# Plain attention pairs whose value product is turned round, and weight words that are joined from contiguous operands

## Chip, core and metric

The kernel runs on one core of a Trainium2 chip. The metric is the device time of one execution in microseconds (us), and the median of three runs is what counts. The profile is one execution of the same program, so every duration below belongs to that execution.

## What is computed

Attention over 4 batches, 8 heads, 768 positions and a head size of 64, in which a query sees the first 4 keys and the 128 keys that end at its own position, followed by a feed-forward block over all 3072 tokens:

```python
def _attn_ref(q, k, v, n_sink, window):
    scores = np.matmul(q, k.transpose(0, 1, 3, 2)) / np.sqrt(D)
    keep = is_sink | in_window
    scores = np.where(keep, scores, -1000000000.0)
    a = np.exp(scores - np.max(scores, axis=-1, keepdims=True))
    a = a / (np.sum(a, axis=-1, keepdims=True) + 1e-09)
    return np.matmul(a, v)

def _moe_ref(x, w_in, w_out):            # 512 -> 2048 -> 512
    h = x @ w_in
    g = h * np.clip(h + 3.0, 0.0, 6.0) / 6.0
    return g @ w_out
```

The feed-forward weights arrive as 64-bit floats, the rest as 32-bit floats.

## The kernel before

**Tiling.** The tokens are cut into 12 units of 256 (4 batches, 3 units each). The four units that begin a batch come first, as units 0 to 3. Of a unit, attention is done for one pair of heads at a time, so there are 48 pairs. The first 14 pairs are "plain": their products run on 32-bit floats as they are. All other products use a float split into a high and a low part, and three products of the parts.

**A plain pair** `s` goes through these steps, and each has a letter. `S` computes the scores of two query tiles (`t`) for both heads (`h`) on TensorE. `M` (line 370) applies the mask on VectorE (DVE) and finds the row's least value. `X` (line 404) takes the exponential on ScalarE (ACT), which also adds up each row by an accumulator. `R` (lines 409 and 410) adds 1e-9 to the two sums of a head and inverts them on DVE. `N` (lines 395 and 397) scales the 128x128 or 128x256 block of probabilities by the inverse, on DVE, or on ACT where the string `NORM0` says so (only for `h` = `t` = 1). `T` (line 443) transposes three 128x128 blocks on TensorE and `C` copies them to SBUF (DVE or ACT by the string `PFE`). `E` (line 495) multiplies with the values: the values are the stationary operand, padded with zeros to 128 columns so that both heads add up in one tile `av` of 128 features by 256 tokens, and the probabilities move past. `x` and `y` (lines 552 and 556) write the high and low part of `av`, the input of the feed-forward block.

**The weights.** Each of the 16 halves of weight tiles (`W`, `w`) arrives as pairs of 32-bit words and is put together into floats of 128x1024 in six steps: ACT takes the high words (1) and the low words (2), DVE joins them in two bitwise instructions (3, line 199, and 4, line 202), then the high part is copied (5, ACT or DVE) and the low part is subtracted (6, line 207, DVE). Before, step 2 writes back in place, so both joins read and step 3 writes every second 32-bit word.

**The feed-forward block** of a unit has 8 slices: `F` (line 576, 24 matmuls a slice in two halves), `G` (four steps on ACT and DVE that end in line 603) and `O` (line 618, 12 matmuls in two halves).

**The order.** A long string `FIRST` lists, step by step, the first part of the program: pairs 0 to 11, pair 12 up to `C`, all 16 weight halves, and the feed-forward blocks of units 0 and 1. Each engine executes its steps in that order. After it comes a loop over the other pairs that spreads the feed-forward work of the other units between their steps. `keep_busy` (step `i`, line 86) issues matmuls that compute nothing; ten stand at the program's start and 17 more in `FIRST`. PSUM tiles come from a pool of eight banks.

Of the kernel before, what the change touches and what calls it, by code (L numbers as in the profile page):

```python
# [44 lines left out]
def attn_ffn_kernel(ctx: ExitStack, tc: tile.TileContext, qx, kx, vx, px, vsx, limits, w_in, w_out, out):  # L45
# [127 lines left out]
    def W_decode(j, step):  # L173
# [14 lines left out]
        if step == 1:  # L188
# [21 lines left out]
    GHF = "DDDDADDADADDDAAD"  # L210
    WHI = "AAAADDAAADAAAAAD"
# [45 lines left out]
    PFE = "AAADAAADADAAAAAAAADADADAAA"  # L257
    XHF = "DAAAAAAAADAAA"
# [4 lines left out]
    homes = {}  # L263

    def A_lent(s):
# [4 lines left out]
        nc.sync.dma_start(out=home, in_=px[b, p])  # L270
        st_[s].update(kr=home[:, 0:256], qr=home[:, 256:512],
                      VS=home[:, 512:1024].rearrange("p (t h d) -> p t h d", t=2, h=2))
# [9 lines left out]
    def A_v(s):  # L282
        b, u, p = pus[s]
        n = 3 if u else 2
        if plain(s):
            VS = work.tile([P, 2, 2, 2 * D], F32, tag="VS", name="VF")
            nc.sync.dma_start(out=VS.rearrange("p t h d -> p (t h d)"), in_=px[b, p][:, 512:1024])
# [103 lines left out]
    NORM0, NORM = "AADDAAAADAADA", "AAAA"  # L391
# [9 lines left out]
    def X_exp(s, h, t):  # L401
        d, i = st_[s], 2 * h + t
        blk = cell(s, h, t, 0, spans(pus[s][1])[t][1])
        nc.scalar.activation(out=blk, in_=blk, func=AF.Exp, scale=-1.0,  # L404
                             bias=d["nb"][:, i:i + 1], accum_out=d["sm"][:, i:i + 1])

# [4 lines left out]

    def N_plain(s, h, t):
        i = 2 * h + t
        norm(NORM0[s % len(NORM0)] if i == 3 else "D", cell(s, h, t, 0, spans(0)[t][1]), st_[s]["rc"][:, i:i + 1])

    def C_soft(s, h):
# [3 lines left out]
        for t in range(2):  # L420
            X_exp(s, h, t)
        R_sums(s, h)
# [67 lines left out]
    def E_plain(s, h):  # L490
        d = st_[s]
        if h == 0:
            d["av"] = ps.tile([P, UT], F32, tag="bank", name="av")
        for slot, c, o0 in ((0, 0, 0), (1, 2 * P, P)):
            nc.tensor.matmul(out=d["av"][:, o0:UT], lhsT=d["VS"][:, slot, h, :], rhs=d["pf"][:, h, c:c + UT - o0],  # L495
                             start=(h == 0 and slot == 0), stop=(h == 1 and slot == 1))

    def E_av(s, h):
# [4 lines left out]
        if plain(s):  # L503
            E_plain(s, h)
            if h == 1:
                x_high(s, d["av"])
                x_low(s, d["av"])
# [150 lines left out]
    def drain(n):  # L658
# [15 lines left out]
        p.0 p.1 W.0 p.2 p.3 W.1 p.4 p.5 p.6 S.0.0 p.7 S.0.1 M.0.0.0 W.2 M.0.1.0 X.0.0.0 M.0.0.1 S.1.0 W.3 S.1.1  # L674
        i.10 X.0.1.0 M.0.1.1 X.0.0.1 M.1.0.0 m W.4 M.1.1.0 M.1.0.1 W.5 X.0.1.1 R.0.0 l.8 X.1.0.0 M.1.1.1 X.1.0.1
        N.0.0.0 N.0.0.1 R.0.1 X.1.1.0 T.0.0 R.1.0 N.0.1.1 N.0.1.0 N.1.0.0 N.1.0.1 X.1.1.1 T.0.1 T.1.0 C.0.0
        R.1.1 C.0.1 E.0.0 N.1.1.0 N.1.1.1 w.0.1 S.2.0 S.2.1 M.2.0.0 E.0.1 M.2.1.0 w.0.2 M.2.0.1 M.2.1.1 S.3.0
        x.0 X.2.0.0 S.3.1 w.0.3 X.2.0.1 T.1.1 i.7 X.2.1.0 X.2.1.1 R.2.0 M.3.0.0 C.1.0 N.2.0.0 N.2.0.1 X.3.0.0
        R.2.1 E.1.0 w.1.1 M.3.0.1 N.2.1.0 T.2.0 N.2.1.1 M.3.1.0 T.2.1 M.3.1.1 X.3.0.1 S.4.0 y.0 X.3.1.0 C.1.1
        S.4.1 X.3.1.1 R.3.0 E.1.1 M.4.0.0 w.1.2 N.3.0.0 N.3.0.1 R.3.1 T.3.0 M.4.0.1 C.2.0 N.3.1.0 S.5.0 N.3.1.1  # L680
        C.2.1 M.4.1.0 E.2.0 M.4.1.1 X.4.0.0 w.0.4 X.4.0.1 T.3.1 X.4.1.0 E.2.1 X.4.1.1 R.4.0 W.6 M.5.0.0 S.5.1
        x.1 N.4.0.0 x.2 C.3.1 C.3.0 y.2 X.5.0.0 S.6.0 y.1 E.3.0 w.0.5 N.4.0.1 R.4.1 M.5.0.1 T.4.0 N.4.1.0
        N.4.1.1 E.3.1 M.5.1.0 M.5.1.1 X.5.0.1 T.4.1 w.1.3 x.3 S.6.1 C.4.0 X.5.1.0 S.7.0 y.3 X.5.1.1 C.4.1 E.4.0
        w.2.2 R.5.0 R.5.1 N.5.0.0 N.5.0.1 E.4.1 N.5.1.1 N.5.1.0 M.6.0.0 w.3.2 M.6.0.1 T.5.0 M.6.1.0 T.5.1
        M.6.1.1 S.7.1 w.0.6 x.4 C.5.0 C.5.1 E.5.0 X.6.0.0 y.4 X.6.0.1 w.1.4 F.0.0.0 X.6.1.0 X.6.1.1 R.6.0 W.7
# [292 lines left out]
```

## Time and profile before

| | |
|---|---|
| median of 3 runs | 667.37 us (665.54 to 667.58) |
| the profiled execution's own time | 666.84 us |
| its span in the trace | 665.0 us |
| TensorE matmul (PE) busy | 652.1 us, 98% of the span |
| VectorE (DVE) busy | 516.0 us, 78% |
| ScalarE (ACT) busy | 413.2 us, 62% |
| chain of work that ended last | PE 83%, DVE 14% |

A matmul's busy time runs to its modelled end, and matmuls overlap: a matmul of 256 columns is shown with some 277 ns, although the next one starts much sooner. So the busy share of PE says little, and the pace, from start to start, says how much work PE has. The same holds on DVE and ACT to a smaller degree. The chain of waits, which is printed in order of time, shows such paces.

### The profile page before, as it was taken

To read this page: it belongs to the slowest core of one execution; us is meant where nothing else is said; L and a number is where in the kernel's file an instruction comes from. 1 tells how busy PE (TensorE), PEld (TensorE's weight loads), DVE (VectorE), ACT (ScalarE), POOL (GpSimd) and SP (SyncE) were. 2 spreads that over 40 slices of the span, in tenths; PEclk is the share of its full clock that TensorE was granted. 3 is DMA by queue.
4 is the path that set the end of the run, shared out by engine and by line. 5 is a ranking of instruction groups with operands and counts; after the bars stand their busy time and mean duration, and the time that the engine had idled before them with its cause. 6 is when DMAs were issued, how large, how long until landed. Compare 5 with 4: busy or idle time off the path is not lost.

```text
span 665.0 us, 13749 instructions
## 1 busy us (share of the span) xinstructions
PE 652.1 (98%) x4594; PEld 611.8 (92%) x4594; DVE 516.0 (78%) x1433; ACT 413.2 (62%) x1042; POOL 181.1 (27%) x336
## 2 busy tenths in 40 slices
PE   9999999999999999999999999999999999999995
PEld 7779889889999999999999999999999999999994
DVE  6999999656779878887887887977986987875431
ACT  6997795365566666666666567667666666662211
POOL 1000000000034353344433533443443435332000
PEclk9999999999999999999999999999999999999998
DMA  8940750045455545455456446545544454420001
GB/s 332 380 160 32 285 222 17 17 131 136 122 144 142 147 121 151 114 143 162 119 123 171 110 119 167 132 110 146 145 129 131 126 146 121 108 66 1 33 1 36
DMA packets 47646, 86.45 MB, mean 130 GB/s; under 512 B 7632, under 2 KB 31952, under 8 KB 45520
## 3 DMA queue, kind: packets, MB, share of 16 engines
q1 hardware_dynamic: 47568, 85.49, 44.2%
q8 instruction: 39, 0.64, 0.4%
q14 instruction: 39, 0.32, 0.1%
HBM read 42.99 MB, written 6.29 MB: 74 GB/s over the span
## 4 chain that ended last, share of the span: by engine, by line
PE 83%; DVE 14%; issue 1%; ACT 0%; POOL 0%; POOLq 0%; ACTq 0%
PE hps L576 34%; PE o L618 34%; PE av L524 6%; PE sp L388 5%; DVE wt L202 3%; PE pt L461 2%; DVE w L207 2%; DVE lent L199 2%; DVE Ph L370 2%; DVE Ph L397 1%; DVE g L603 1%; DVE st L199 1%; PE av L495 1%; DVE gf L594 1%; PE idle L86 1%
## 5 line engine op out<-in xcount | busy, mean ns | idle before, releaser
L576 PE MATMUL hps<-x,w 128*128 128x256 f32 x2304 | 282.4, 277 | 2.0 <-ACT pf L35 0.9
L576 PEld LDWEIGHTS hps<-x,w 128*128 128x128 f32 x2304 | 269.4, 192 | 5.8 <-ACT pf L35 1.3
L618 PE MATMUL o<-w,gh 128*128 128x512 f32 x768 | 234.0, 386 | 0.0
L428 POOL TENSOR_TENSOR Pt<-Pt 128x256 f32<-128x256 f32 x64 | 53.9, 842 | 355.1 <-ACT Pt L404 355.1
L618 PEld LDWEIGHTS o<-w,gh 128*128 128x128 f32 x768 | 139.6, 197 | 9.9 <-issue 0.7
L618 PE MATMUL o<-w,g 128*128 128x512 f32 x384 | 145.9, 380 | 1.0 <-DVE g L603 0.8
L589 ACT ACTIVATE gf<-hps,three 128x512 f32<-128x512 f32 x96 | 66.3, 691 | 82.6 <-PE hps L576 82.4
L594 DVE SCALAR_TENSOR_TENSOR gf<-gf,hps 128x512 f32<-128x512 f32 x96 | 66.5, 695 | 35.7 <-ACT gf L589 34.0
L618 PEld LDWEIGHTS o<-w,g 128*128 128x128 f32 x384 | 75.4, 196 | 9.6 <-DVE g L603 2.1
L474 POOL TENSOR_SCALAR_AFFINE_SELECT ph<-ph 128x256 fp32r<-128x256 f32 x128 | 63.7, 498 | 41.0 <-ACT ph L35 41.0
L404 ACT ACTIVATE Pt<-Pt,nb 128x272 f32<-128x272 f32 (+2 forms) x136 | 69.9, 514 | 8.0 <-DVE nb L370 7.4
L395 ACT ACTIVATE Pt<-Pt,rc 128x144 f32<-128x144 f32 (+2 forms) x136 | 49.3, 410 | 35.8 <-DVE rc L410 34.6
L476 POOL TENSOR_SCALAR_AFFINE_SELECT ph<-ph 128x256 fp32r<-128x256 f32 x128 | 64.9, 507 | 23.0 <-DVE ph L30 17.6
L370 DVE CUSTOM_DVE_ANT_0 Pt<-sp,m_t 128x272 f32<-128x272 f32 x128 | 53.2, 433 | 22.9 <-PE sp L388 18.7
L603 DVE TENSOR_TENSOR g<-gf,gh 128x512 fp32r<-128x512 f32 x96 | 69.2, 723 | 1.0
L30 DVE TENSOR_TENSOR kt<-kr,kt 128x400 fp32r<-128x400 f32 (+1 forms) x34 | 21.9, 643 | 27.5 <-DMA out_dram<-ost 14.6
L388 PE MATMUL sp<-K 128*128 128x272 f32 (+2 forms) x272 | 42.6, 279 | 0.0
L524 PE MATMUL av<-ph,VS 128*128 128x256 f32 x268 | 40.9, 275 | 0.0
L41 DVE CAST gh<-gf 128x512 fp32r<-128x512 f32 x91 | 39.6, 436 | 1.3
L388 PEld LDWEIGHTS sp<-K 128*128 128x128 f32 x272 | 38.3, 190 | 1.2
L409 DVE TENSOR_SCALAR sm<-sm 128x2 f32<-128x2 f32 x96 | 32.9, 343 | 7.4 <-ACT Pt L404 6.8
L30 DVE TENSOR_TENSOR ph<-pt,ph 128x256 fp32r<-128x256 f32 (+1 forms) x68 | 29.0, 426 | 11.4 <-ACT ph L35 10.9
(95 smaller groups left out, 794.4 us busy)
## 6 DMA issues: line engine op xcount, KB each, us to landing
K<-kt SPq DMA_DIRECT2D x128, 200.0 KB, 3.5
K<-kt SPq DMA_DIRECT2D x136, 64.0 KB, 2.5
kr<-in_kx_dram SPq DMA_DIRECT2D x32, 200.0 KB, 2.5
out_dram<-ost SPq DMA_DIRECT2D x48, 128.0 KB, 2.1
vr<-in_vx_dram SPq DMA_DIRECT2D x32, 192.0 KB, 2.6
lent<-in_w_in_dram SPq DMA_DIRECT2D x5, 1024.0 KB, 10.6
lent<-in_w_out_dram SPq DMA_DIRECT2D x5, 1024.0 KB, 12.4
qr<-in_qx_dram SPq DMA_DIRECT2D x40, 128.0 KB, 2.3
```

What stands on the lines that cost most here:

```text
L370: nc.vector.tensor_tensor_reduce(out=cell(s, h, t, 0, w), in0=sp[:, 0:w], in1=m[:, 0:w], scale=-SCALE, scalar=3.0e38, op0=ALU.add, op1=ALU ...
L388: nc.tensor.matmul(out=sp[:, 0:w], lhsT=Q[:, h, t * P:(t + 1) * P], rhs=keys, start=(r == 0), stop=(r == 1))
L404: nc.scalar.activation(out=blk, in_=blk, func=AF.Exp, scale=-1.0, bias=d["nb"][:, i:i + 1], accum_out=d["sm"][:, i:i + 1])
L428: nc.gpsimd.tensor_tensor(out=both, in0=both, in1=prior, op=ALU.add)
L474: nc.gpsimd.affine_select(out=prior[i], in_=own[i], pattern=[[0, 2], [-1, P]], base=0, channel_multiplier=1, compare_op=ALU.is_gt, fill=0.0)
L476: nc.gpsimd.affine_select(out=own[i], in_=own[i], pattern=[[0, 2], [1, P]], base=0, channel_multiplier=-1, compare_op=ALU.is_ge, fill=0.0)
L524: nc.tensor.matmul(out=o, lhsT=l, rhs=r, start=(j == 0), stop=(j == len(seq) - 1))
L576: nc.tensor.matmul(out=hp[:, half, :], lhsT=l(i)[:, c, fs], rhs=r, start=(c == 0 and j == 0), stop=(c == NP - 1 and j == 2))
L589: nc.scalar.activation(out=gf, in_=hp, func=AF.Relu, bias=three, scale=1.0)
L594: nc.vector.scalar_tensor_tensor(out=gf, in0=gf, scalar=6.0, in1=hp, op0=ALU.min, op1=ALU.mult)
L603: eng(GLO, state["n"] * NP).tensor_tensor(out=g, in0=gf, in1=gh.bitcast(F32), op=ALU.subtract)
L618: nc.tensor.matmul(out=acc, lhsT=l[:, f, tt::2], rhs=r(i)[:, f, :].rearrange("p (s d) -> p d s", s=2), start=(i == 0 and f == 0 and j == 0 ...
```

## The change

The change has three parts and a new table.

1. For plain pairs the transposed probabilities become the stationary operand of `E`, and the values move: 65 columns for one head, the 65th being all ones, so that column 64 of the result is the row's sum. The exponential no longer accumulates. `R` now runs once for a pair, on the four sums in PSUM. A new step `U` scales the result (128x256) by the inverses on DVE, and a new step `V` transposes it back on TensorE (two 128x128 blocks into a PSUM tile `xp`), from which `x` and `y` read. `N` is gone. The packed input of a pair is 772 words wide instead of 1024, and for pairs 0 and 1 it is loaded in two pieces (`q`, `u`).
2. Of the weights, step 1 keeps the sign of the high word (`Copy` for `Abs`), step 2 writes to a contiguous tile `last`, and both joins read and write contiguous words. `last` lies in the second half of the place that the finished weights will take.
3. `FIRST` is written anew, without step `i`. It holds the same pairs, weight halves and feed-forward slices as before. The strings that choose engines change too: over the plain pairs `x` stands on DVE for 8 instead of 3, and one copy of each kind (`C`, weight step 5, `G` step 3) changes sides.

```diff
-            nc.scalar.activation(out=d["it"].bitcast(F32), in_=high.bitcast(F32), func=AF.Abs, scale=2.0 ** -112)
+            nc.scalar.activation(out=d["it"].bitcast(F32), in_=high.bitcast(F32), func=AF.Copy, scale=2.0 ** -112)
...
-            nc.scalar.activation(out=low, in_=low.bitcast(U32), func=AF.Copy, scale=2.0 ** -29 * (1 - 2.0 ** -18),
-                                 bias=7.5 * 2.0 ** -18 - 0.5)
+            d["last"] = lent(NW - 1 - j, I32)[:, PW:2 * PW]
+            nc.scalar.activation(out=d["last"], in_=low.bitcast(U32), func=AF.Copy,
+                                 scale=2.0 ** -29 * (1 - 2.0 ** -18), bias=7.5 * 2.0 ** -18 - 0.5)
         elif step == 3:
-            nc.vector.scalar_tensor_tensor(out=low, in0=high, scalar=-2 ** 31, in1=low,
+            nc.vector.scalar_tensor_tensor(out=d["last"], in0=d["it"], scalar=-2 ** 31, in1=d["last"],
                                            op0=ALU.bitwise_and, op1=ALU.bitwise_or)
         elif step == 4:
-            nc.vector.scalar_tensor_tensor(out=d["it"], in0=d["it"], scalar=3, in1=low,
+            nc.vector.scalar_tensor_tensor(out=d["it"], in0=d["it"], scalar=3, in1=d["last"],
                                            op0=ALU.logical_shift_left, op1=ALU.bitwise_or)
...
-    PFE = "AAADAAADADAAAAAAAAADADADAAA"
-    XHF = "DAAAAAAAADAAA"
+    PFE = "DAAAADDADAAAAAAAADAAAAADAA"
+    XHF = "DDDAADDDAAAA"
...
+    def R_plain(s):
+        d = st_[s]
+        nc.vector.tensor_scalar(out=d["sm"], in0=d["av"][:, :, D], scalar1=1e-9, scalar2=None, op0=ALU.add)
+        nc.vector.reciprocal(out=d["rc"], in_=d["sm"])
+
+    def U_plain(s):
+        d = st_[s]
+        d["rows"] = work.tile([P, 2, 2, D], F32, tag="tmp", name="rows", bufs=1)
+        nc.vector.tensor_tensor(out=d["rows"].rearrange("p t h d -> p h t d"),
+                                in0=d["av"][:, :, 0:D].rearrange("p (h t) d -> p h t d", h=2),
+                                in1=d["rc"].rearrange("p (h t) -> p h t", h=2).unsqueeze(3).to_broadcast([P, 2, 2, D]),
+                                op=ALU.mult)
+
+    def V_plain(s):
+        d = st_[s]
+        d["xp"] = ps.tile([P, UT], F32, tag="bank", name="xp")
+        for t in range(2):
+            nc.tensor.transpose(out=d["xp"][:, t * P:(t + 1) * P],
+                                in_=d["rows"][:, t].rearrange("p h d -> p (h d)"), identity=ident)
...
-    def N_plain(s, h, t):
-        i = 2 * h + t
-        norm(NORM0[s % len(NORM0)] if i == 3 else "D", cell(s, h, t, 0, spans(0)[t][1]), st_[s]["rc"][:, i:i + 1])
...
-            d["av"] = ps.tile([P, UT], F32, tag="bank", name="av")
-        for slot, c, o0 in ((0, 0, 0), (1, 2 * P, P)):
-            nc.tensor.matmul(out=d["av"][:, o0:UT], lhsT=d["VS"][:, slot, h, :], rhs=d["pf"][:, h, c:c + UT - o0],
-                             start=(h == 0 and slot == 0), stop=(h == 1 and slot == 1))
+            d["av"] = ps.tile([P, 4, D1], F32, tag="bank", name="av")
+        for t in range(2):
+            for slot in range(t + 1):
+                c = (t + slot) * P
+                nc.tensor.matmul(out=d["av"][:, 2 * h + t, :], lhsT=d["pf"][:, h, c:c + P], rhs=d["VS"][:, slot, h, :],
+                                 start=(slot == 0), stop=(slot == t))
...
     FIRST = """
-        p.0 p.1 W.0 p.2 p.3 W.1 p.4 p.5 p.6 S.0.0 p.7 S.0.1 M.0.0.0 W.2 M.0.1.0 X.0.0.0 M.0.0.1 S.1.0 W.3 S.1.1
+        q.0 q.1 p.2 u.1 u.0 v.9 W.2 p.3 p.4 S.0.0 W.0 S.0.1 M.0.0.0 p.5 S.1.1 M.0.1.0 X.0.0.0 M.0.1.1 S.1.0
...
```

The program's order, on TensorE behind the ten `idle` matmuls at the start, where the scores of pairs 0 and 1 end. `idle` are matmuls that compute nothing, `sp` are scores, `pt` the transposed probabilities (`Ph`); `lent` and `ident_r` hold a pair's inputs and the identity. Before:

```order
L357 MATMUL sp_148<-lent_108 128x256
L357 MATMUL sp_150<-lent_108 128x256
L86 MATMUL idle_152<-ident_r_72 128x128 x10
L443 MATMUL pt_198<-ident_r_72,Ph_132 128x128 x3
L443 MATMUL pt_209<-ident_r_72,Ph_132 128x128 x3
```

After, at the same place:

```order
L359 MATMUL sp_145<-lent_108 128x128
L359 MATMUL sp_147<-lent_108 128x128
L466 MATMUL pt_163<-ident_r_72,Ph_132 128x128 x3
L466 MATMUL pt_178<-ident_r_72,Ph_132 128x128 x3
L359 MATMUL sp_184<-lent_111 128x256
L359 MATMUL sp_186<-lent_111 128x256
```

The ten `idle` matmuls ahead of the first transposes are gone, so the transposes stand right behind the scores.

On DVE, where one pair's sums stand among the work of others (`nb` holds a pair's least values, `sm` and `rc` its sums and their inverses, `pf` the copied transposes, `av` the product with the values, `rows` the scaled product; `st` holds the words of a weight half as they were loaded). Before, with pairs 6 and 7:

```order
L202 SCALAR_TENSOR_TENSOR wt_292<-wt_292,st_116 128x1024
L409 TENSOR_SCALAR sm_449<-sm_449 128x2
L410 RECIPROCAL rc_450<-sm_449 128x2
L370 ISA Ph_502,nb_503<-sp_426,m_00_100 128x128
L370 ISA nb_503 128x1
L397 TENSOR_SCALAR Ph_447<-Ph_447,rc_450 128x128
L397 TENSOR_SCALAR Ph_447<-Ph_447,rc_450 128x256
```

After, with pairs 3, 4 and 6:

```order
L41 COPY pf_384<-pt_335 128x384
L414 TENSOR_SCALAR sm_279<-av_341 128x4
L415 RECIPROCAL rc_280<-sm_279 128x4
L200 SCALAR_TENSOR_TENSOR lent_333<-wt_352,lent_333 128x1024
L420 TENSOR_TENSOR rows_408<-av_341,rc_280 128x2x2x64
L203 SCALAR_TENSOR_TENSOR wt_352<-wt_352,lent_333 128x1024
L372 ISA Ph_420,nb_421<-sp_389,m_00_100 128x128
```

The two sums of one head, with the scaling of its probabilities behind them, have become four sums that are read from the product `av`, with one scaling of that product behind them. The joins read and write `wt` and `lent` (which is `last` here), both contiguous, where one of them read `st`, of which it took every second word.

On TensorE, where the products of a pair stand among the work of others. Before, with pairs 1 to 5:

```order
L495 MATMUL av_289<-pf_282,lent_108 128x256
L495 MATMUL av_289<-pf_282,lent_108 128x128
L443 MATMUL pt_334<-ident_r_72,Ph_277 128x128 x3
L357 MATMUL sp_342<-lent_118 128x128
L357 MATMUL sp_344<-lent_118 128x128
L495 MATMUL av_349<-pf_339,lent_113 128x256
L495 MATMUL av_349<-pf_339,lent_113 128x128
```

After, with pairs 3 to 6 (`xp` are the new transposes of step `V`):

```order
L520 MATMUL av_341<-lent_111,pf_327 128x65 x3
L359 MATMUL sp_379<-lent_167 128x256
L359 MATMUL sp_381<-lent_167 128x256
L359 MATMUL sp_387<-lent_167 128x128
L359 MATMUL sp_389<-lent_167 128x128
L466 MATMUL pt_394<-ident_r_72,Ph_364 128x128 x3
L520 MATMUL av_400<-lent_120,pf_384 128x65 x3
L466 MATMUL pt_404<-ident_r_72,Ph_364 128x128 x3
L520 MATMUL av_400<-lent_120,pf_384 128x65 x3
L429 MATMUL xp_414<-ident_r_72,rows_408 128x128 x2
```

A product of one head has three matmuls of 65 columns instead of one of 256 and one of 128. Between the last product of pair 3 (`av_341`) and its transposes back (`xp_414`) stand scores, transposes and products of later pairs.

## Rows read from the trace of the kernel before

**Rows 1.** Busy time in stretches: start:end, length; PE, PEld, DVE, ACT, POOL busy (instructions); PEclk, DMA share, GB/s.
```profile
6.00:26.00 20.00, 19.75 (x146) 16.12 (x147) 17.82 (x93) 19.02 (x60) 0.20 (x1) 1.00 1.02 424
26.00:46.00 20.00, 18.71 (x122) 14.78 (x119) 19.73 (x70) 19.82 (x54) 0.00 (x0) 1.00 0.50 195
86.00:106.00 20.00, 19.11 (x125) 16.43 (x123) 19.93 (x35) 15.59 (x23) 0.00 (x0) 1.00 0.37 143
```

**Rows 2.** Chain of waits in order of time: start us, us, engine, tile, line, count.
```profile
104.92 1.14 DVE w L207
106.10 5.40 PE hps L576 x46
```

**Rows 3.** Groups by line and form, 0 to 230 us: busy us, mean ns, idle before.
```profile
L207 DVE TENSOR_TENSOR w<-wt,w 128x1024 fp32r<-128x1024 f32 x16 | 20.2, 1277 | 0.0
L199 DVE SCALAR_TENSOR_TENSOR lent<-lent 128x1024 int32<-128x1024 int32 x10 | 14.2, 1448 | 0.0
L202 DVE SCALAR_TENSOR_TENSOR wt<-wt,lent 128x1024 int32<-128x1024 int32 x10 | 13.8, 1414 | 0.0
L404 ACT ACTIVATION_READ_ACCUMULATOR Ph<-Ph,nb 128x1 f32 x56 | 11.4, 203 | 0.0
L397 DVE TENSOR_SCALAR Ph<-Ph,rc 128x128 f32<-128x128 f32 x26 | 7.2, 280 | 0.1
L397 DVE TENSOR_SCALAR Ph<-Ph,rc 128x256 f32<-128x256 f32 x17 | 5.9, 347 | 0.0
L395 ACT ACTIVATE Ph<-Ph,rc 128x256 f32<-128x256 f32 x11 | 5.5, 503 | 0.4 <-DVE rc L410 0.3
```

**Rows 4.** DVE in order of time: start us, us, line, operation, tiles, count.
```profile
28.23 0.15 DVE L409 TENSOR_SCALAR sm<-sm 128x2 f32<-128x2 f32 x1
28.42 0.17 DVE L410 RECIPROCAL rc<-sm 128x2 f32<-128x2 f32 x1
28.50 0.72 DVE L397 TENSOR_SCALAR Ph<-Ph,rc 128x128 f32<-128x128 f32 x3
```

**Rows 5.** Chain of waits: pieces on DVE, which show its paces.
```profile
14.41 1.22 DVE st L199
16.10 0.46 DVE Ph L397 x2
18.19 0.34 DVE x L556
18.52 0.47 DVE pf L41
46.44 2.70 DVE lent L199 x2
89.82 0.60 DVE w L41
```

**Rows 6.** Chain of waits: pieces on PE, which show its paces.
```profile
130.80 0.65 PE av L495 x4
136.09 2.60 PE o L618 x12
142.12 0.66 PE pt L443 x6
142.78 2.68 PE hps L576 x24
145.46 0.86 PE sp L357 x8
159.12 0.63 PE sp L388 x6
```

**Rows 7.** PE in order of time at the start: start us, us, line, tiles, count.
```profile
1.21 4.63 PE L86 MATMUL idle<-rel 128*128 128x128 f32 x20 [1.21 <-POOL rel L65]
7.77 2.50 PE L86 MATMUL idle<-ident_r 128*128 128x128 f32 x20
```

**Rows 8.** Busy time in the last stretch, behind the last matmul; columns as in rows 1.
```profile
662.00:665.00 3.00, 0.00 (x0) 0.00 (x0) 0.00 (x0) 0.00 (x0) 0.00 (x0) 0.50 0.01 3
```

More of the change, by code (lines that the diff above doesn't have):

```diff
@@ L263, in attn_ffn_kernel, with A_lent @@
     homes = {}
-    def A_lent(s):
+    D1 = D + 1
+    def A_lent(s, c0=0, c1=2 * UT + 4 * D1):
         b, u, p = pus[s]
@@ L269, in A_lent @@
         home = homes[s // 2][:, 1024 * (s % 2):1024 * (s % 2 + 1)]
-        nc.sync.dma_start(out=home, in_=px[b, p])
+        nc.sync.dma_start(out=home[:, c0:c1], in_=px[b, p][:, c0:c1])
         st_[s].update(kr=home[:, 0:256], qr=home[:, 256:512],
-                      VS=home[:, 512:1024].rearrange("p (t h d) -> p t h d", t=2, h=2))
+                      VS=home[:, 512:512 + 4 * D1].rearrange("p (t h d) -> p t h d", t=2, h=2))
     def A_kq(s):
@@ L285, in A_v @@
         if plain(s):
-            VS = work.tile([P, 2, 2, 2 * D], F32, tag="VS", name="VF")
-            nc.sync.dma_start(out=VS.rearrange("p t h d -> p (t h d)"), in_=px[b, p][:, 512:1024])
+            VS = work.tile([P, 2, 2, D1], F32, tag="VS", name="VF")
+            nc.sync.dma_start(out=VS.rearrange("p t h d -> p (t h d)"), in_=px[b, p][:, 512:512 + 4 * D1])
             st_[s]["VS"] = VS
@@ L389, in C_score @@
         S_least(s, h, t, sp)
-    NORM0, NORM = "AADDAAAADAADA", "AAAA"
+    NORM = "AAAA"
     def norm(e, blk, c):
@@ L403, in X_exp @@
         blk = cell(s, h, t, 0, spans(pus[s][1])[t][1])
+        if plain(s):
+            nc.scalar.activation(out=blk, in_=blk, func=AF.Exp, scale=-1.0, bias=d["nb"][:, i:i + 1])
+            return
         nc.scalar.activation(out=blk, in_=blk, func=AF.Exp, scale=-1.0,
                              bias=d["nb"][:, i:i + 1], accum_out=d["sm"][:, i:i + 1])
+    def R_plain(s):
[15 more added lines that the diff above has]
+                                in_=d["rows"][:, t].rearrange("p h d -> p (h d)"), identity=ident)
     def R_sums(s, h):
@@ L421, in C_soft @@
             X_exp(s, h, t)
+        if plain(s):
+            return
         R_sums(s, h)
@@ L505, in E_av @@
             if h == 1:
-                x_high(s, d["av"])
-                x_low(s, d["av"])
+                R_plain(s)
+                U_plain(s)
+                V_plain(s)
+                x_high(s, d["xp"])
+                x_low(s, d["xp"])
             return
@@ L716, in attn_ffn_kernel @@
-    pair = {"S": S_plain, "X": X_exp, "R": R_sums, "N": N_plain, "T": T_plain, "C": T_copy, "E": E_plain,
-            "p": A_lent, "l": A_kq, "v": A_v, "W": W_load, "w": W_decode}
+        q.0 q.1 p.2 u.1 u.0 v.9 W.2 p.3 p.4 S.0.0 W.0 S.0.1 M.0.0.0 p.5 S.1.1 M.0.1.0 X.0.0.0 M.0.1.1 S.1.0
+        X.0.1.0 l.8 M.0.0.1 X.0.1.1 M.1.1.1 X.0.0.1 M.1.0.1 T.0.1 p.6 X.1.1.1 M.1.0.0 m M.1.1.0 T.0.0 p.7
+        X.1.0.1 S.2.1 W.4 C.0.1 C.0.0 X.1.1.0 W.3 S.2.0 X.1.0.0 E.0.0 M.2.0.1 v.8 M.2.1.0 X.2.0.1 M.2.1.1 T.1.0
@@ new lines, in attn_ffn_kernel @@
+        x.6 F.0.1.0 M.9.0.0 y.6 R.7 M.9.1.0 X.9.0.0 U.7 w.4.1 M.9.0.1 V.7 M.9.1.1 T.8.0 x.7 T.8.1 G.0.0.2
+        F.0.1.1 X.9.0.1 X.9.1.1 C.8.1 X.9.1.0 y.7 C.8.0 T.9.1 w.4.3 E.8.0 T.9.0 G.0.0.3 w.1.1 E.8.1 w.4.4
+        F.1.0.0 w.1.2 v.10 R.8 l.10 G.0.0.4 C.9.0 F.1.1.0 U.8 l.11 C.9.1 w.1.3 G.0.1.1 W.11 w.5.2 E.9.0 G.0.1.2
+        V.8 E.9.1 w.1.4 w.4.5 F.1.1.1 R.9 x.8 w.1.5 F.1.0.1 y.8 U.9 w.1.6 S.10.0 G.1.0.1 S.10.1 w.4.6 w.3.1 V.9
+        O.0.0.1 M.10.1.0 M.10.0.1 x.9 M.10.0.0 W.9 X.10.1.0 M.10.1.1 S.11.1 w.6.1 v.11 y.9 G.1.0.2 S.11.0
@@ new lines, in attn_ffn_kernel @@
+        G.0.7.1 O.0.6.0 G.1.5.4 G.0.7.2 G.1.6.1 O.1.5.1 G.1.6.2 O.1.5.0 O.0.6.1 G.1.6.3 G.1.6.4 F.1.7.1 G.0.7.3
+        G.0.7.4 O.1.6.0 G.1.7.1 G.1.7.2 O.1.6.1 O.0.7.1 G.1.7.3 G.1.7.4 O.0.7.0 o.0.1 O.1.7.1 o.0.0 O.1.7.0
+        o.1.1 o.1.0
+    """
+    pair = {"S": S_plain, "X": X_exp, "R": R_plain, "U": U_plain, "V": V_plain, "T": T_plain, "C": T_copy, "E": E_plain,
+            "p": A_lent, "q": lambda s: A_lent(s, 0, 2 * UT), "u": lambda s: A_lent(s, 2 * UT), "l": A_kq, "v": A_v, "W": W_load, "w": W_decode}
@@ L937, in _layout @@
             vx[:, u, :, :, j] = vp[:, :, T * t:T * (t + 1)]
-    vfx = _np.zeros((B, NP, T, 2, 2, 2, D), v.dtype)
-    for h in range(2):
-        vfx[:, :, :, :, h, h] = vp[:, :, 0:2 * T, h].reshape(B, NP, 2, T, D).transpose(0, 1, 3, 2, 4)
+    vfx = _np.ones((B, NP, T, 2, 2, D + 1), v.dtype)
+    vfx[..., 0:D] = vp[:, :, 0:2 * T].reshape(B, NP, 2, T, 2, D).transpose(0, 1, 3, 2, 4, 5)
     vsx = _np.zeros((B, 8, 16, NP, 2, D), v.dtype)
```

77 lines of the change are left out of this document (31 added, 46 removed).

## Prediction

> **What bounds the kernel now.** I first read the busy time in stretches [rows 1]. PE seems full everywhere, but a matmul's busy time runs past the start of the next one, so I look at DVE. It works 19.7 to 19.9 of every 20 us in two of the three stretches between 26 and 106 us, and 17.8 in the stretch from 6. ACT is nearly as full up to 46 us (19.0 and 19.8). Then I read the chain of waits in order of time [rows 2]: up to 106.0 us it runs over DVE almost alone, the last piece being the low part of a weight half, and from 106.1 us on it runs over PE to the end. So the planned part, the string FIRST, is bound by DVE for its first 106 us and by PE behind that, and the loop that follows by PE throughout. Whatever is saved in the planned part passes to the end, as long as PE can use it.
>
> How much can PE use? Its work in the planned part, by paces [rows 6, 7]: 384 matmuls of the first product are 16 times the 2.68 us of 24, which is 42.9; 192 of the second are 16 times 2.60, 41.6; 24 products of a head at 0.65 are 15.6; 78 transposes at 0.11 (six took 0.66) are 8.6; scores of 13 pairs at 0.86 are 11.2; 34 matmul records that compute nothing are about 3.7, by 20 in 2.50 with the tail of the last taken off. Together 123.6 us. The part ends with the transposes of pair 12, which stand at 142.1 to 142.8 [rows 6], and PE's real work begins at 5.8, where the first ten fillers end [rows 7]. That is 137.0 us for 123.6 of work: 13.4 us in which PE waited. **This is the purse**; more than this can't be gained unless PE's own work shrinks.
>
> **The change part by part: DVE.** Scalings (N) that go: 17 of 256 columns and 26 of 128 [rows 3]. One of each takes 0.46 at DVE's pace [rows 5], and by their means of 280 and 347 ns [rows 3] the small one has 0.21 of it. So 17 x 0.46 + 9 x 0.21 = 9.7 us saved. Sums (R): a pair had two, each 28.50 - 28.23 = 0.27 us from start to start [rows 4]; now one. 14 x 0.27 = 3.8 saved; I price the new one like the old, since its four elements are as small, and its reading from PSUM is within the upper bound of U below. Scaling of the product (U): added 14 times, 256 elements from PSUM and one from SBUF. No such row exists; the nearest is the low part of x, 256 elements from PSUM and SBUF, 0.34 [rows 5]. The lower bound is the scaling of 256 elements in SBUF, 0.46 - 0.21 = 0.25; the upper 0.34 plus one R of 0.27, in case it has to wait for the inverses right in front of it, 0.61. I take 0.34: 4.8 added, between 3.5 and 8.5. Moved copies: x stands on DVE 5 times more, 5 x 0.34 = 1.7, one copy of transposes 0.47, one high part of a weight half 0.60 [rows 5]; one copy of G goes, which I leave out. 2.8 added.
>
> Joins: 32 bitwise instructions on 128x1024 words that now read and write contiguous words. Before they took 1448 and 1414 ns in their larger groups; the subtraction of the low part, the same size but contiguous, took 1277 [rows 3]. If they come down to that, 16 x 0.171 + 16 x 0.137 = 4.9 us are saved. The bounds are 0 and this; I take 4.9, because the subtraction runs among the same neighbours.
>
> The earliest join paces at 1.22 us, before the feed-forward matmuls begin, and a later pair of joins at 2.70 / 2 = 1.35 [rows 5], so the strided form costs something only at some times. [...]
>
> DVE's sum: -9.7 - 3.8 + 4.8 + 2.8 - 4.9 = **-10.8 us**, between -2.2 (dear U, joins unchanged) and -12.1 (cheap U).
>
> **ACT** loses 56 accumulator reads (203 ns each [rows 3], of which about half overlaps the neighbour), 11 scalings of 0.50 and five of the copies of x; it gains nothing but one copy of G. About 12 us come off an engine that was full until 46 us, so it does not take DVE's place. Step 2 of the weights still reads every second word, so I leave it as it is. The load of a pair shrinks from 1024 to 772 words. DMA is busy throughout the first stretch [rows 1], so this helps rather than hurts; the loads were ahead of the scores already, and I price it at nothing. Its cover is the ten fillers and the scores of two pairs; without it a late load would show as a wait of the scores.
>
> **PE.** A head's product changes from 4 records (two of 256 columns, two of 128) to 6 records of 65 columns. By columns alone a record would take 65/128 of a transpose's 0.11, so 0.056. But six records of the loop's scores, four of 128 and two of 256 columns in a cheaper format, took 0.63, so 0.105 each, while 24 of 256 columns in that format took 0.112 each [rows 6]: below some length a record costs 0.105 whatever its columns, which I put down to the load of 128 stationary columns that each brings. I take 0.105 to 0.11: 6 x 0.108 = 0.65 a head, exactly what it was. Between 0.34 and 0.65 a head, this is a gain of 0 to 7 us of PE's work. The transposes back (V) add 12 x 2 x 0.11 = 2.6 in the planned part, the fillers that go save 3.7. PE's work becomes 122.5 us.
>
> **A wait that is added.** V needs U, which needs R, which needs the last product, so PE hands each pair to DVE once more. Unhidden, that is R 0.27, U 0.34 with its tail, and PE's way back, some 0.9 us. In the new order 1.7 to 3.4 us of other PE work stand between a pair's last product and its V (the third place shown above: four scores, two transposes, two products). So I price it at nothing on PE alone. What remains is that PE and DVE now have nearly equal work, and a small mismatch stops one of them.
>
> **The sum.** From the purse: PE's own work gives a floor of 5.8 + 122.5 = 128.3 for the end of the planned part. The first transposes need the first exponentials; fillers stood there and now nothing does, about 2.5 us of the 7.77 to 10.27 that they covered [rows 7], so 130.8. DVE's bound, 10.8 us off 142.8, is 132.0. Two in-order engines that are level will not reach the larger of two bounds; I add 1.5 us for that, which is a judgement: 12 new hand-offs at 0.12. The end comes at 133.5, that is 9.3 us earlier. From the profiled execution's own 666.84 this makes 657.5; that execution lies 0.5 below the median of 667.37, so the median should be **658.0 us**. The loop is bound by PE before and after, so nothing is given back there; what is late next is PE itself.
>
> **The rivals.** *Hand-offs eat it.* If each of the 12 new hand-offs shows 0.4 us, 5 us go, and the time is 663. For it: PE, DVE and ACT are all near full at 26 to 46 us [rows 1]. Against it: the order's cover. *Joins unchanged.* The change does not do what it says: DVE saves 5.9, the time is 658 + 4.9 = 663 at most, less if PE would have stopped it anyway; about 662. *More than forecast.* Records of 65 columns at less than 0.105 and no mismatch: 653. [...]
>
> [...]
>
> **How the numbers follow.** Forecast of 655 to 661.5: 0.56. Hand-offs or joins, 661.5 to 665.3: 0.23. Below 655: 0.09. No change, for a mixture of these with a short fall of the clock, 665.4 to 669.4: 0.07. The clock, above: 0.05. A measurement of this kernel tells 0.3%, about 2 us, from no change. Faster by over that: 0.56 + 0.23 + 0.09 = 0.88; same 0.07; slower 0.05. The range of 8 in 10 is 653.5 to 664.5, which leaves out about 0.05 below and 0.15 above.
>
> **What would show it.** In the profile after, the joins should take some 1.28 us, U some 0.4, and a head's product 0.65 on PE; the planned part should end at about 133.5 instead of 142.8, and the chain should go over to PE well before 106 us. If the joins stay at 1.4, that term is wrong; if PE's new products pace at 0.06, the purse was larger; if the granted clock of the first 30 us is below 1.00, the fillers were needed; if PE waits for `rows` or `pf` throughout, the hand-offs were. The prediction is wrong if the planned part ends later than 140.

## The result, and the profile after

| | before | after |
|---|---|---|
| median | 667.46 us (665.54 to 667.58, 4 runs) | 656.89 us (656.04 to 657.34, 4 runs) |
| profiled execution, its span | 666.84, 665.0 us | 657.34, 655.5 us |
| PE, DVE, ACT busy | 652.1, 516.0, 413.2 us | 645.4, 504.0, 399.9 us |

The ratio is 0.9847, with a 95% interval of 0.9826 to 0.9867: 10.2 us faster, give or take 1.4. A second set, beside the last experiments, gave 656.15 us (655.66 to 657.17) and 0.9851 (0.9837 to 0.9864). The forecast was 658.0.

The busy time in stretches of the kernel after, which answers [rows 1] (start:end, length; PE, PEld, DVE, ACT, POOL busy; PEclk, DMA share, GB/s):

```profile
6.00:26.00 20.00, 19.54 (x170) 16.88 (x167) 17.40 (x83) 16.90 (x39) 0.20 (x1) 1.00 0.98 396
26.00:46.00 20.00, 19.84 (x176) 18.49 (x175) 19.49 (x60) 18.12 (x33) 0.00 (x0) 1.00 0.77 300
86.00:106.00 20.00, 20.00 (x148) 19.29 (x148) 19.96 (x23) 18.06 (x18) 0.00 (x0) 1.00 0.00 1
```

PE does more in the same time: 176 instead of 122 matmuls between 26 and 46 us. A part of that is only that a head's product has six records instead of four, but 72 of them instead of 36 belong to the feed-forward block. ACT is less full up to 46 us (16.90 and 18.12 instead of 19.02 and 19.82; 16.28 and 19.08 in the second profile below). DVE is about as full as it was, in the same stretches, although it has less to do: its work comes earlier. The granted clock is 1.00 in all of them.

The groups of the kernel after that answer [rows 3], from 0 to 230 us (busy us, mean ns, idle before):

```profile
L200 DVE SCALAR_TENSOR_TENSOR lent<-wt,lent 128x1024 int32<-128x1024 int32 x16 | 19.5, 1218 | 1.2 <-ACT wt L192 0.9 <-ACT lent L197 0.2
L203 DVE SCALAR_TENSOR_TENSOR wt<-wt,lent 128x1024 int32<-128x1024 int32 x16 | 19.5, 1217 | 0.0
L208 DVE TENSOR_TENSOR w<-wt,w 128x1024 fp32r<-128x1024 f32 x16 | 19.3, 1216 | 0.2
L420 DVE TENSOR_TENSOR rows<-av,rc 128x256 f32<-128x256 f32 x14 | 5.9, 418 | 0.1
```

The joins fell from 1448 and 1414 ns to 1218 and 1217, below the 1277 that the low part took before; and the low part, which was not changed, fell to 1216 too. The new scaling `rows` takes 418 ns.

In this profile the chain of waits breaks off after its last piece. So here is the chain of a second profiled execution of the same kernel (span 653.9 us), in order of time (start us, us, engine, tile, line, count):

```profile
18.86 0.62 PE av L520 x6
19.49 0.24 PE xp L429 x2
19.75 0.42 DVE x L41
...
22.57 1.11 DVE lent L200
23.69 0.33 DVE rows L420
...
38.19 0.35 DVE rows L420
38.58 0.44 PE xp L429 x2
39.02 0.66 PE pt L466 x6
...
124.12 7.78 PE o L646 x36
131.90 2.68 PE hps L604 x24
```

This is the picture of the whole change. Before, the chain ran over DVE up to 106.0 us [rows 2]; now it does so from 19.75 to 38.58 only, and PE carries it on both sides of that. The 24 matmuls of the first product with which the loop begins started at 142.78 [rows 6]; they start at 131.90: 10.9 us earlier. From there to the end this execution takes 522.0 us and that of the kernel before 522.2 (in the first profile of the kernel after, whose loop starts 0.1 us earlier, it is some 1.7 us more).

### The profile page after: what moved, and what is told of

The parts are those of the page before. It is cut to its first block, busy times and chain, and to the rows that moved or that the text cites. A ratio compares the mean times of both kernels' runs of the same rounds, so it can differ in the third digit from the quotient of the medians.

```text
span 655.5 us, 13752 instructions
## 1 busy us (share of the span) xinstructions
PE 645.4 (98%) x4644; PEld 612.5 (93%) x4644; DVE 504.0 (77%) x1382; ACT 399.9 (61%) x967; POOL 181.0 (28%) x336
## 5 line engine op out<-in xcount | busy, mean ns | idle before, releaser
L41 DVE CAST gh<-gf 128x512 fp32r<-128x512 f32 x90 | 38.1, 423 | 4.0 <-PE o L646 2.7
L35 ACT ACTIVATE ph<-pt 128x256 fp32r<-128x256 f32 (+1 forms) x68 | 26.4, 388 | 18.0 <-PE pt L484 17.4
```

## The experiments

| kernel | median us (range) | ratio to before, 95% | start of the loop in its trace |
|---|---|---|---|
| after, again | 656.15 (655.66 to 657.17) | 0.9851 (0.9837 to 0.9864) | 131.9 |
| after, strided joins | 659.97 (659.54 to 660.46) | 0.9898 (0.9880 to 0.9915) | 135.0 |
| after, with fillers | 659.79 (659.29 to 660.15) | 0.9886 (0.9861 to 0.9911) | 3.4 later than after |
| after, more on DVE | 662.30 (660.67 to 662.60) | 0.9927 (0.9902 to 0.9952) | 136.1 |
| after, with accumulators | 659.72 (658.20 to 660.59) | 0.9903 (0.9888 to 0.9919) | 134.4 |
| after, less on DVE | 655.97 (655.67 to 656.54) | 0.9843 (0.9830 to 0.9857) | 131.6 |
| before, no scaling | 663.08 (662.25 to 663.37) | 0.9945 (0.9929 to 0.9962) | 138.6 |
| before, contiguous joins | 664.70 (663.92 to 666.65) | 0.9970 (0.9959 to 0.9980) | 2.5 earlier than before |
| before, both | 661.94 (661.45 to 662.21) | 0.9919 (0.9894 to 0.9944) | 138.6 |
| before, no fillers | 667.74 (667.13 to 668.83) | 1.0007 (0.9996 to 1.0017) | 1.2 later than before |
| the change in the old order | 682.79 (679.42 to 686.40) | 1.0263 (1.0232 to 1.0294) | 12.3 later than before |

They were run in three sets on three chips, each set with its own runs of before (medians 666.95, 666.94 and 666.43). Kernels of different sets are compared by their ratios; 0.001 is 0.67 us. The start of the loop is read from one execution each; where the chain of waits breaks off, PE's records in order of time give the difference.

### Is the price of the joins that of the kernel or of one execution?

The kernel before once more, without an edit.

> The kernel before, unchanged, for a second trace of it on the chip that the other runs use. If the joins' price belongs to the kernel, the two joins take 1.41 to 1.45 us again and the contiguous subtraction 1.28; if it belonged to that one trace, all three come to 1.22 as in the kernel after. Time 667.5.

It took 666.24 us. One group of its joins:

```profile
L199 DVE SCALAR_TENSOR_TENSOR lent<-lent 128x1024 int32<-128x1024 int32 x10 | 14.0, 1422 | 0.0
```

1422 against 1448 ns in [rows 3], and 1250 for the low part against 1277. The price belongs to the kernel, to within some 2%.

### The strided joins alone, put back

```diff
-            d["last"] = lent(NW - 1 - j, I32)[:, PW:2 * PW]
+            d["last"] = lent(NW - 1 - j, I32).rearrange("p (n w) -> p n w", w=2)[:, :, 1]
```

> The kernel after, with one edit: the tile for the low words takes every second word, so that both joins read and write a step of 8 bytes again; order and everything else stay. Theory (the step costs DVE time, and DVE still shares the bound): joins 1.35 to 1.45 us instead of 1.22, 16 x 2 x 0.15 = 5 us more on DVE, of which 2.5 to 5 reach the end: 659.5 to 662 against 656.9. [...]

0.9898 against 0.9849, the mean of the two sets of after: 3.3 us come back, and the loop starts 3.1 us later. The first joins up to 60 us, and from 60 to 130 us:

```profile
L200 DVE SCALAR_TENSOR_TENSOR lent<-wt,lent 128x1024 int32<-128x1024 int32 x6 | 7.7, 1284 | 0.0
```

```profile
L200 DVE SCALAR_TENSOR_TENSOR lent<-wt,lent 128x1024 int32<-128x1024 int32 x10 | 15.1, 1509 | 0.9 <-ACT wt L192 0.8
```

The same line of the kernel after, from 60 to 130 us:

```profile
L200 DVE SCALAR_TENSOR_TENSOR lent<-wt,lent 128x1024 int32<-128x1024 int32 x10 | 12.2, 1218 | 1.0 <-ACT wt L192 0.8
```

A step of 8 bytes costs little in the first joins (1284 ns) and a quarter more later (1509 ns), where PE streams the feed-forward matmuls; contiguous words cost 1214 ns up to 60 us in the second profile of the kernel after, and 1218 from 60 to 130. In this kernel's chain DVE holds on and off until 113.8 us. So without this part of the change about 3 us are lost, of the 5.9 us that it takes off DVE here (joins and low parts). The theory held.

### The scaling alone, taken away in the old order

The kernel before without the steps `N` of pairs 0 to 12 in `FIRST`:

```diff
-        N.0.0.0 N.0.0.1 R.0.1 X.1.1.0 T.0.0 R.1.0 N.0.1.1 N.0.1.0 N.1.0.0 N.1.0.1 X.1.1.1 T.0.1 T.1.0 C.0.0
+        R.0.1 X.1.1.0 T.0.0 R.1.0 X.1.1.1 T.0.1 T.1.0 C.0.0
...
```

> The kernel before with the scalings N of pairs 0 to 12 left out, so that these probabilities stay unscaled; the old order, fillers and joins stay. Theory (DVE's relief alone pays, while PE has waits left): 9.7 us come off DVE in the planned part, 7 to 9.7 of them reach the end: 658 to 660.5. Rival (the new order or the missing fillers pay, not DVE): 665.5 to 667.5.

9.7 us off DVE gave 3.9 us: neither the theory's 7 to 9 nor the rival's nothing. What is late next stands in its chain of waits:

```profile
35.34 0.87 ACT Ph L404 x4
36.21 1.11 ACT lent L196
...
38.37 0.99 ACT Ph L404 x4
...
40.22 1.22 ACT wt L192
41.44 1.00 ACT lent L196
```

Between 26 and 51 us it runs mainly over ACT, with its exponentials and its steps of the weights. From 50.8 us on it is DVE's again, with the joins and low parts of the weights, until PE takes over at 102.8.

### The contiguous joins alone, in the old order

```diff
-            nc.vector.scalar_tensor_tensor(out=low, in0=high, scalar=-2 ** 31, in1=low,
+            nc.vector.scalar_tensor_tensor(out=d["st"][:, 0:PW], in0=d["st"][:, PW:2 * PW], scalar=-2 ** 31, in1=d["st"][:, 0:PW],
...
-            nc.vector.scalar_tensor_tensor(out=d["it"], in0=d["it"], scalar=3, in1=low,
+            nc.vector.scalar_tensor_tensor(out=d["it"], in0=d["it"], scalar=3, in1=d["st"][:, 0:PW],
```

> The kernel before with both joins on contiguous halves of the staged words, so the joined words are not the weights; order, waits and all else stay. Theory: 16 x 2 joins fall from 1.44 to 1.22 to 1.28 us, 4.9 us come off DVE and 4 to 4.9 reach the end: 662.5 to 663.5. Rival (the joins' cost is hidden or not from the step): 666 to 667.5.

```profile
L207 DVE TENSOR_TENSOR w<-wt,w 128x1024 fp32r<-128x1024 f32 x16 | 19.4, 1216 | 0.0
L202 DVE SCALAR_TENSOR_TENSOR wt<-wt,lent 128x1024 int32<-128x1024 int32 x10 | 12.0, 1220 | 0.5 <-ACT wt L192 0.5
L199 DVE SCALAR_TENSOR_TENSOR lent<-lent 128x1024 int32<-128x1024 int32 x10 | 12.0, 1217 | 0.2 <-ACT wt L192 0.2
```

Joins of contiguous words take 1217 to 1220 ns in the old order too, and the low part drops to 1216 although nothing in it was edited. But only 2.0 us reach the end by the ratio, and 2.5 us the start of the loop, of the 7 to 8 that the groups' means give.

### Both at once, in the old order

> The kernel before, in its old order, with two parts of the change at once: pairs 0 to 12 leave out the scaling of their probabilities, and the joins work on contiguous words (the joined words are then not the weights). DVE loses about 9.7 + 4.9 = 14.6 us, more than in the whole change. Alone, the two parts gave 3.9 and 2.3 us. Theory now, 'the order lets through what PE can use': the two together give their sum, 6.2 us, so about 660.7 (659.8 to 661.6), and the last 4 us of the change need the new order. Rival, 'enough relief is enough': DVE goes off the path as a whole and the time falls to that of the change, 656.5 to 658.5. Rival, 'the old order is exhausted': both parts free the same waits of PE, no more than the larger alone, 662.3 to 663.5.

5.0 us by the medians, 5.4 by the ratio (its interval is 3.7 to 7.1). In the traces the loop starts at 138.63 here and at 138.60 with the scaling away alone. So the joins added between nothing and 1.7 us, and the runs don't decide between the theory's sum and the rival "exhausted"; the rival "enough relief is enough" fails. Three pieces of the chain of waits:

```profile
30.89 1.34 PE hps L576 x12
...
44.72 2.83 PE hps L576 x12
...
71.20 10.66 DMA lent<-in_w_in_dram
```

Twelve matmuls of the same kind took 1.34 us and then 2.83, and the granted clock of this profile is 0.97 in the stretch from 26 to 46 us and 0.94 in the next, against 1.00 in the others up to 146 us. So its start of the loop is no clean measure. (The other three executions of this kernel, with a mean clock of 0.996 to 0.998, took 661.45 to 662.21 us, so the clock is not what keeps the time up.) The load began at 71.20 us, and its half of a weight was waited for until 81.9. DVE lost more busy time in this kernel (125.4 to 115.4 us, from 6 to 146 us) than in the whole change (121.6), and the time fell about half as far. **DVE's relief does not explain the other 5 us.**

### The fillers, taken out of before and put into after

The kernel before without `i.10` and `i.7`:

> The kernel before without the 17 steps of matmuls that compute nothing (34 records) which stand in its string; the ten at the program's start stay. Theory now, 'they stood where PE waits anyway': 666.0 to 667.5, no change, and PE waits longer in front of the first transposes. Rival, 'they were work on the path': 3.7 us of PE's work go, 663.3 to 664.5. Rival, 'the clock needs them': the granted clock falls below 1.00 between 6 and 26 us, 670 or more.

No gain: 0.5 us slower, with an interval that reaches to no change. PE at the start, and the busy time in four stretches:

```profile
9.29 0.61 PE L443 MATMUL pt<-ident_r,Ph 128*128 128x128 f32 x3 [1.54 <-DVE Ph L397]
```

```profile
8.00:10.00 2.00, 0.61 (x3) 0.34 (x3) 1.90 (x13) 1.76 (x9) 0.05 (x1) 1.00 0.97 399
10.00:12.00 2.00, 1.72 (x8) 1.36 (x9) 1.21 (x6) 2.00 (x7) 0.00 (x0) 0.85 1.07 444
12.00:14.00 2.00, 2.00 (x11) 1.27 (x9) 0.51 (x4) 2.00 (x3) 0.00 (x0) 0.50 0.97 406
14.00:16.00 2.00, 2.00 (x14) 1.41 (x12) 1.33 (x6) 1.55 (x7) 0.00 (x0) 0.80 1.03 420
```

PE waits 1.54 us for the first transposes and is busy 0.61 us between 8 and 10 us. The granted clock is 0.85 in the next stretch, 0.50 from 12 to 14 us, and 0.80 from 14 to 16. In the kernel before, with the fillers, it is 1.00 there [rows 1]. The fillers stood in a wait, and with them the clock stayed at 1.00.

The same steps put into the kernel after (`i.10` ahead of `T.0.1`, `i.7` ahead of `E.1.0`):

> The kernel after with the same 17 steps of matmuls that compute nothing put back: ten in front of the second transposes of pair 0, seven in front of the second product of pair 1. They are 2.5 and 1.75 us of PE's time. Theory now, 'they cost where PE does not wait': PE waits some 2.2 us in the first 20 us and 2.7 in the next, and the fillers lie partly in these waits: plus 1 to 2.5 us, 658 to 659.5. Rival, 'the fillers are the missing gain': all of it shows, plus 3.7 to 4.3 us, 660.6 to 661.2. Rival, 'free': 656.5 to 657.5.

The loop starts 3.4 us later, and by ratios 2.5 us come back, of the expected 2.5 + 1.75 = 4.25 us of fillers: the upper end of what the theory gave. In the new order they stand mostly in PE's way.

### Time put on DVE, and taken off it, in the kernel after

```diff
-            nc.vector.tensor_tensor(out=part(j)[:, 1], in0=like(d["it"].bitcast(F32)),
-                                    in1=part(j)[:, 0].bitcast(F32), op=ALU.subtract)
+            for _ in range(2 if j in (2, 0, 1, 4) else 1):
+                nc.vector.tensor_tensor(out=part(j)[:, 1], in0=like(d["it"].bitcast(F32)),
+                                        in1=part(j)[:, 0].bitcast(F32), op=ALU.subtract)
```

> The kernel after with the low part of four early weight halves (2, 0, 1 and 4) computed twice: 4 x 1.22 = 4.9 us more on DVE, before some 40 us, and nothing else. Theory now, 'DVE and PE are level in the planned part': about half shows, plus 2 to 3.2 us, 659 to 660.2, since the strided joins, 6 us of DVE's time, showed 3.1. Rival, 'PE alone bounds the planned part now': plus 0 to 1 us, 656.5 to 658. Rival, 'DVE still bounds it up to 106 us': all of it shows, plus 4.3 to 5 us, 661.2 to 662.

All of it shows, within the noise: 5.2 us by ratios (3.5 to 6.9), 4.2 in the start of the loop. The theory of half was wrong for this direction.

The other direction leaves out the addition of 1e-9 in `R_plain`:

```diff
-        nc.vector.tensor_scalar(out=d["sm"], in0=d["av"][:, :, D], scalar1=1e-9, scalar2=None, op0=ALU.add)
-        nc.vector.reciprocal(out=d["rc"], in_=d["sm"])
+        nc.vector.reciprocal(out=d["rc"], in_=d["av"][:, :, D])
```

> The kernel after with the inverses taken from the product's sums at once, without the addition of 1e-9 ahead of them (each sum holds the exponential of zero, so it is at least 1, and 32-bit floats don't change by 1e-9 there). 14 small instructions go from DVE, at 0.13 us each by their pace: 1.8 us, of which 1.2 stand ahead of 56 us. Theory now, 'DVE's time in the first third reaches the end nearly whole': minus 0.6 to 1.4 us, 655.3 to 656.2. Rival, 'PE is as full': within 0.4 us of after.

0.2 us below after in the same set by the medians and 0.5 by the ratios, which is within the noise, and the loop starts 0.3 us earlier. The time alone would not exclude the low end of the theory. The chain of waits in the stretch that DVE held in the kernel after says more:

```profile
22.18 1.49 issue
...
28.36 1.28 ACT wt L192
...
29.66 0.33 SPq L168
...
30.04 0.42 SPq L280
...
30.51 5.40 DMA qr<-in_qx_dram
...
36.05 0.93 PE sp L359 x8
36.98 1.53 PE hps L603 x12
38.51 0.22 PE xp L428 x2
```

DVE is gone from it. In the first piece ACT does nothing for 1.49 us, and the profile shows no wait for it. ACT frees the place that a weight half is loaded into at 29.64 us; the load of that half (line 168) is issued at 29.66; the queries of a pair stand behind it in SyncE's queue and take 5.40 us; and the chain comes to the transposes back at 38.51, where it came at 38.58 by way of DVE. In the kernel after, four of the additions stand between the copy of `x` at 19.75 us, where the chain goes over to DVE, and the one at 36.77, a stretch of 17.02 us. By their pace there (0.19 us, from 22.21 to 22.40) they are an estimated 0.8 us of it. Without them the chain waits for the queries instead, and the scores that need these start at 36.05 only. The two chains end together. More time on DVE costs all of it; less gives next to nothing. The rival held, though it named PE and it is ACT and a load.

### The accumulators, put back into the kernel after

```diff
-            nc.scalar.activation(out=blk, in_=blk, func=AF.Exp, scale=-1.0, bias=d["nb"][:, i:i + 1])
+            nc.scalar.activation(out=blk, in_=blk, func=AF.Exp, scale=-1.0, bias=d["nb"][:, i:i + 1],
+                                 accum_out=spare[:, i:i + 1])
```

> The kernel after with the accumulation of each plain exponential put back, into a tile that nobody reads: 56 accumulator reads of 203 ns on ACT, 11.4 us of busy time, about half of it on ACT's pace. DVE and PE do the same as after. Theory now, 'ACT had to be relieved as well': with DVE's scaling and strided joins gone in the old order, the chain between 26 and 50 us ran over ACT; so 1.5 to 4 us come back, 658.2 to 660.8. Rival, 'ACT is off the path': 656.3 to 657.5.

3.6 us come back in the same set, and the loop starts 2.5 us later. The chain of waits goes over to ACT:

```profile
32.99 1.09 ACT Ph L409 x4
34.08 1.18 ACT lent L197
...
40.48 1.09 ACT wt L192
41.56 1.36 ACT Ph L409 x6
42.97 0.55 PE pt L469 x3
```

This is about as much as any single part of the change gave in these runs (3.9 us for the scaling in the old order, 3.3 for the joins in the new), on an engine whose relief the prediction had counted at nothing.

### The kernel after once more, for its chain

> The kernel after once more, to stand beside the other three runs and for its chain of waits. Expected: 656.3 to 657.3. Theory now, 'DVE bounds its first third, PE the rest': the chain goes over to PE for good between 55 and 63 us, where it does with four low parts doubled (55.8). Rival, 'level up to the end of the weights': it goes back to DVE until about 105 to 118 us, where the last low parts are.

The time is as expected. The chain goes over to PE at 38.58 us, earlier than either theory said. DVE is busy 19.6 to 19.9 of every 20 us from 26 to 106 us, and nobody on the chain waits for it.

### The whole change in the old order

The string of before without `N`, `i` and the old sums; `R`, `U` and `V` put in between a pair's last product and its `x`; and 15 steps of weights moved behind the steps that they need with the new tile `last`. For pair 0:

```diff
-        E.0.1 M.2.1.0 w.0.2 M.2.0.1 M.2.1.1 S.3.0 x.0
+        E.0.1 M.2.1.0 w.0.2 R.0 U.0 M.2.0.1 M.2.1.1 S.3.0 V.0 x.0
```

> The whole change in the old order: the string of the kernel before without the scalings, the two sums and the fillers; the new sums and scaling stand halfway between a pair's last product and its copy x, the transposes back right ahead of x, and 15 steps of weights moved behind the steps that they now need. The strings that choose engines are those of after. Theory now, 'the new order collects what the relief alone does not': no better than the two parts of the relief in the old order, 661 to 664. Rival, 'the order is not needed, DVE and ACT relieved together are enough': 656.5 to 659. A third, 'the new hand-offs need their places in the new order': 664.5 to 669, since U and V then stand where PE has little to do.

16 us slower than before by the medians (17.5 by the ratio), beyond all three expectations, with less work on DVE and ACT than before. Its waits from 6 to 130 us (engine, line, waited for: us, times, longest), and the busy time in two stretches:

```profile
DVE lent L200 <- ACT wt L192: 5.5, 4, 2.3
...
PE o L646 <- DVE g L631: 4.9, 3, 3.9
PE xp L429 <- DVE rows L420: 4.3, 6, 1.1
```

```profile
118.00:122.00 4.00, 1.19 (x9) 0.79 (x7) 3.93 (x4) 1.91 (x3) 0.00 (x0) 1.00 0.00 0
122.00:126.00 4.00, 2.90 (x7) 2.35 (x8) 4.00 (x7) 1.32 (x2) 0.00 (x0) 0.58 0.00 0
```

Three things can be seen. PE waits 4.3 us in front of six of the transposes back, which is the rival of the hand-offs, at up to 1.1 us each. The moved steps of weights make PE wait 3.9 us at once for `g`, at 119.2 us, behind four joins on DVE. And right after that wait the granted clock is 0.58 in a stretch of 4 us, where it was 1.00 in the one before. The executions with the lowest mean clock were the longest (0.977 in the one of 686.40, 0.994 in the one of 679.42). How the 16 us divide among the three isn't settled, and since my own placing of `R`, `U`, `V` and the moved steps is part of it, this run shows that the parts don't fit the old order as I put them there. It doesn't show that the old one could not have been adapted with less loss.

## Why the prediction was right, point by point

**The purse** held. 13.4 us of PE waiting stood in the planned part, PE still begins at 5.84 us in the second profile (5.30 in the first), and by the forecast's own 122.5 us of work the wait that is left is 131.9 - 5.8 - 122.5 = 3.6 us. The forecast left 5.2. That is the 1.6 us in the start of the loop by which the change did better; against the median it was 1.1 us, and 1.9 in the second set. Where the 3.6 us lie can be estimated from the chain: outside the stretch from 19.75 to 38.58 us it runs over PE, for 13.9 and 93.3 us, which leaves 122.5 - 107.2 = 15.3 us of PE's work for the 18.8 us of that stretch. So nearly all of the wait that is left stands where DVE holds the chain.

**The wait of the first transposes was the step that failed on PE's side.** I gave it 2.5 us, since fillers had covered as much. PE at the start of the kernel after:

```profile
5.30 1.58 PE L359 MATMUL sp<-lent 64*128 64x128 f32 x16
7.00 1.15 PE L466 MATMUL pt<-ident_r,Ph 128*128 128x128 f32 x6
```

The transposes start 0.12 us behind the scores' end. In the old order without fillers PE did wait (1.54 us, for a scaling of line 397); in the new one no sums or scalings of pairs 0 and 1 stand ahead of them. I read from the old order a wait that belonged to the old order.

**The joins** were right in kind and too small: 16 x (1448 - 1218) + 16 x (1414 - 1217) ns = 6.8 us instead of 4.9, plus 1.0 for a low part that I had held constant. The rival of unchanged joins fell by the run with the step put back: its first joins took 1284 ns before 60 us and 1509 behind it, against 1214 and 1218 with contiguous words.

**The scaling `U`** was priced at 0.34 and paces at 0.33 to 0.35 in the chain, although one shows 418 ns. **A head's product** was priced at 0.65 and paces at 0.62 for six records of 65 columns, 0.103 each (0.81 right behind scores), so the bound of 0.056 by columns alone is excluded. **The clock** stayed at 1.00, with PE busy 19.54 of the 20 us from 6 to 26. No run of the kernel after shows the slower clock that has 0.05 in the forecast: in its two profiles, and in those with fillers, with more on DVE and with accumulators, the granted clock is 1.00 in every stretch of 20 us from 6 to 66 us. The old order does show it: without fillers the clock was 0.50 from 12 to 14 us, and twelve matmuls took 2.83 us instead of 1.34 in the profile with both parts, whose clock was 0.97 from 26 to 46 us and 0.94 from 46 to 66.

**ACT, and DVE as the bound, are where the reasoning was wrong though the number was near.** The sum let DVE's 10.8 us pass to the end up to PE's floor, and took ACT's 12 us only as a reason why ACT would not be next. The runs say otherwise. In the old order 9.7 us off DVE gave 3.9, and over 16 gave 5.0; in the chains of these kernels ACT, and in the second a load too, stand in DVE's place for long stretches. In the new one, putting ACT's accumulators back costs 3.6 us, the strided joins 3.3, the fillers 2.5, and 4.9 us on DVE costs 5.2: each alone shows. The time is the latest of several chains that end close together in the new order, and such prices can't be added up. That the forecast's bound of 132.0 for DVE is next to the measured 131.9 is chance, since DVE leaves the chain at 38.6.

**The rivals.** Hand-offs did not eat the gain in the new order: in the second profile PE's only listed wait from 6 to 130 us is one of 0.3 us for a copy on ACT, although the chain goes once from `rows` to the transposes back (38.58 us). In the change put into the old order PE waited 4.3 us for them. No wait in a trace answers to the 1.5 us that I added for hand-offs by judgement. A relief of DVE, ACT and PE together, in an order made for it, is what the runs support; what the order gives by itself, and how much an old order adapted with more care would have kept, is open. The smaller packed input of a pair, its loading in two pieces and the copies that change sides were not tested by themselves. Open too is a version with the loads of a pair's keys and queries ahead of the weight half in SyncE's queue, which the chain of the kernel without the addition points to; it wasn't tried.

## What to carry to other kernels

When an engine is full, look for what is just as late beside it before counting its relief: one run that puts time on it and one that takes time off tell whether it bounds alone (5.2 us back for 4.9 added; 0.2 gained by the medians for some 0.8 removed in the stretch where it held the chain). A wait read from the old order is no term of a new order; price it from what stands ahead of it there. Where operands can be contiguous at no cost, try it, even if the strided form looks free in one part of the trace (in the kernel before the first join paced at 1.22 us; with the step put back into the kernel after the later ones took 1509 ns, against 1218 contiguous).

## What the chip showed that was not expected

In these runs the price of the 8-byte step changed with what ran beside it: the kernel before's first join paces at 1.22 us [rows 5], and the first strided one in the kernel after took 1284 ns on average before 60 us and 1509 behind it. In that later part PE streams the feed-forward matmuls and ACT runs its own strided steps. Two joins of the kernel before, of the same line, tell them apart (pieces of its chain of waits):

```profile
44.52 1.12 DVE wt L202
...
63.25 1.34 DVE wt L202
```

The first paces at 1.12 us; beside it ACT ran a strided step (line 192, from 44.66 us) and PE no feed-forward matmul. The second paces at 1.34; beside it ACT stood idle and PE streamed the second product (line 618). In this kernel the joins that the timeline shows singly are shown with 1.21 to 1.22 us where no feed-forward matmul ran beside them (four, at 14.41, 21.46, 26.02 and 44.44 us), and with 1.42 to 1.77 where the second product did for most of their time. So in these joins the price went with PE's matmuls and not with ACT's steps; by what mechanism isn't shown.

The low part, contiguous in every kernel, took 1277 and 1250 ns in the two profiles of before and 1216 where only the joins were edited; what made it cheaper is not shown. And the clock was low behind a wait of 1.54 us: in the old order without fillers PE was busy 0.61 us from 8 to 10 us, and the granted clock was 0.85 from 10 to 12 and 0.50 from 12 to 14.
